# The second pass's down projection as seven half-size products, with sums of the activations formed on VectorE and GpSimd, in a replanned order

## The chip, the cores and the metric

The kernel runs on one core of a Trainium2 chip. The metric is the device time of one execution in microseconds (us). The engines are called as the profile calls them: PE (TensorE, matmuls; PEld are its weight loads), DVE (VectorE), ACT (ScalarE), POOL (GpSimd), SP (SyncE, which issues the DMAs).

## The reference, cut to what matters

```python
x = A_x                                  # (1, 1, 8192, 448)
xn = _layernorm(x, axis=-1)
s = _A_ref(xn, ...)                      # FFT along the 8192, a complex two-layer block MLP, soft threshold, inverse FFT
g = _silu((_gelu(xn @ w_gate) * (xn @ w_up)) @ w_down)   # w_gate, w_up: 448 x 1792; w_down: 1792 x 448
return x + s * g
```

All is float32 in and out. The kernel splits each float32 operand of a product into two float16 halves, hi and lo, and forms hi·hi + hi·lo + lo·hi: three matmuls for each product.

## The kernel before, in words

There are two strands of work, and both use the PE.

The feed-forward strand (`ffn`, `chunk`) takes the 8192 tokens in 16 chunks of 512 (NG = 16; a chunk is 4 tiles of 128, CH = 4), and the 1792 hidden columns as 14 blocks of 128 in **two passes**: 8 blocks in the first pass (p = 0), 6 in the second (p = 1). The weights of a pass stay in SBUF (`wt` for gate and up, `dw` for down). A chunk goes through its blocks in pairs; a pair is a **unit** (`unit`). A unit makes the gate and up products from the transposed tokens (`xta`, `xtb`, fetched by a transposing DMA) in the PSUM banks `bx` and `by`, already as seven products in place of eight (`PROD`, steps a1 to a7). ACT copies and gelu, DVE additions and `glu` give the hidden values of the unit in float32 (tiles `u` for one half of the tokens, `gl` for the other); ACT casts them to the hi part of `h`, and DVE or POOL subtracts to get the lo part. Then `down` multiplies: for each of the 4 token tiles, each block, three matmuls with 448 columns into a bank `bd`. That is 4·6·3 = 72 matmuls for a chunk of the second pass. The first pass writes its partial result to DRAM (`prt`); the second reads it back (`pt`), adds its own (DVE), takes tanh (ACT), forms the gate (DVE, tile `th`) and writes it to DRAM (`gsp`). In the last chunk the gate goes straight to the output. `ended` is this epilogue.

The spectral strand uses the banks `bf`. Phase 1 is the layer norm and the first DFT stage; phase 2 works on 64 groups (`group`: second DFT stage, the MLP, the first inverse stage; its PE groups are `bf<-sm,y`, `bf<-z,w1t`, `bf<-zs,w1t`, `bf<-w2t,wn`, `bf<-vt,sm`); phase 3 (`tiles3`, PE group `bf<-u,mt`) is the last inverse stage, multiplied with the gate read from `gsp`, added to x and written out.

The order of all instructions is made when the program is built. `Pace` runs every task as a generator, gives each instruction an estimated cost (`cost`) and lets the task go on that is due next; each engine then executes its instructions strictly in the order so found. `B` (class `Either`) gives an operation to DVE or POOL, whichever ends first by the estimates. The constants `END2` and `END3` set the even spacing at which phases 2 and 3 start their pieces. All engine calls go through one helper, so every row of the profile has the same line, L179, and groups are told apart by their tiles.

Of the kernel before, what the change touches and what calls it, by code (L numbers as in the profile page):

```python
# [21 lines left out]
NG = 16  # L22
CH = 4
# [8 lines left out]
K1, K2 = 256, 192  # L32

# [14 lines left out]
class Pace:  # L48
# [4 lines left out]
    def __init__(self):  # L53
        self.now, self.last, self.n, self.heap = 0.0, 0.0, 0, []
        self.free, self.seen, self.dma = {}, {}, 0.0

# [73 lines left out]
    def issue(self, e, op, out, ins, run):  # L130
        outs, ins, start = self.start(e, out, ins)
        if e == "SP":
            self.free[e] = start + 0.5
            size = (outs or ins)[0].nbytes()
            self.dma = max(self.dma, start) + size / 320e3
            end = max(start + 2.2 + size / (170e3 if op == "dma_start_transpose" else 240e3), self.dma + 1.5)
        else:
            end = start + self.cost(e, op, start, out, ins)
            self.free[e] = end
        for i in ins:  # L140
# [4 lines left out]
        return run()  # L145

    def cost(self, e, op, start, out, ins):

        n = max([a.free_size() for a in (out, *ins)])
        if e == "PE":  # L150
            n = out.free_size()
            return max(0.049, n * 0.00042 + 0.001) * (4 if ins[0].dtype == F32 and op == "matmul" else 1)
        if e == "ACT":
            return 0.19 + 0.00086 * n + (0.08 if op != "copy" and n > 128 else 0.0)
        if e == "POOL":
            return 1.1 if n < 8 and op == "tensor_tensor_pow" else 0.2 + 0.0023 * n
        src = [i for i in ins if i.free_size() == n]
        sb = [i for i in src if i.space != bass.MemoryType.PSUM]
        if n < 32:
# [4 lines left out]
        if op == "tensor_scalar" and sb:  # L164
            return 0.15 + 0.0008 * n + min(busy, 0.5)
        return 0.14 + 0.00107 * n
# [34 lines left out]
class Ring:  # L201
# [19 lines left out]
    def put(self, ap):  # L221
# [5 lines left out]
        else:  # L227
            self.free.append(t)

# [96 lines left out]
def afno_geglu_kernel(ctx, tc, x, gu, wd, mlp, b1, b2, c_m, c_mt, c_small, out):  # L326
# [13 lines left out]
    dsp = nc.dram_tensor("dsp", (128, 2, PF[1][1], D), F16, kind="Internal").ap()  # L340
# [87 lines left out]
    YS = ring(p1, [128, 2, 2, D], F16, "ysb", 2)  # L428
# [5 lines left out]
    XTA = ring(fp, [128, XA // 128, 256], F16, "xta", 1)  # L434
# [7 lines left out]
    PT = ring(fp, [128, D], F32, "pt", 2)  # L442
# [84 lines left out]
    def stage1(c, q, xs):  # L527
# [6 lines left out]
        for a in range(2):  # L534
# [7 lines left out]
            S.activation(ysb[:, a, 0, :], py, AF.Copy, scale=2.0 ** -16)  # L542
            yield
            V.scalar_tensor_tensor(ysb[:, a, 1, :], py, 2.0 ** -16, ysb[:, a, 0, :],
                                   op0=ALU.mult, op1=ALU.subtract)
# [3 lines left out]
        for ri in range(2):  # L549
            Q.dma_start(t1[:, ri, n2:n2 + 2, :], ysb[64 * ri:64 * ri + 64].rearrange("p a s d -> p a (s d)"))  # L550
# [57 lines left out]
    def gu_block(b, to):  # L608
# [23 lines left out]
        S.activation(fc[:, 5, b:b + 1], half[:, 1:2], AF.Copy, scale=2.0 ** -25)  # L632
# [73 lines left out]
    def down_weights(p):  # L706
# [4 lines left out]
        else:  # L711
            parts = [(fp0 + k, min(3, nf - k)) for k in range(0, nf, 3)]
# [25 lines left out]
        def split(f, n):  # L738
            t, v = yield from load(f, n)
            if p == 1:  # L740
                do = yield from WO.get()
                dv = do.rearrange("p s v c -> p (s v c)")[:, 0:2 * n * D].rearrange("p (s t c) -> p s t c", s=2, t=n)
            for i in range(n):
                d = [w[:, f + i] for w in dw] if p == 0 else [dv[:, s, i] for s in range(2)]
# [4 lines left out]
                if p == 0:  # L749
                    done("dw", f + i)  # L750
                yield
            (WS if p == 1 else rings[f]).put(t)
            if p == 1:
                Q.dma_start(dsp[:, :, f - fp0:f - fp0 + n, :], dv)
                WO.put(do)
# [18 lines left out]
        V.tensor_scalar(eguv[:, bs], eguv[:, bs], inv, 2.0 ** 14, op0=ALU.mult, op1=ALU.mult)  # L774
        V.tensor_scalar(cB[p], ED, 2.0 ** -11, None, op0=ALU.mult)
# [11 lines left out]
    def far_down():  # L787
        n = PF[1][1]
        for s in range(2):
            Q.dma_start(dw[s][:, 0:n], dsp[:, s])  # L790

    def prep_mlp():

        nonlocal f2, f20, ca, ca0, w1t, w2t, b1s, b2s
# [84 lines left out]
        rm.close()  # L879

# [40 lines left out]
    def glu(p, f0, gl, up, half, h, back):  # L921
        for cs, b in scaled(p, f0):
            V.scalar_tensor_tensor(gl[:, cs], up[:, cs], fc[:, 5, b:b + 1], gl[:, cs],
                                   op0=ALU.mult, op1=ALU.mult)
        back()
        yield
        v = gl.rearrange("p (e c) -> p e c", e=2)
# [5 lines left out]
    def unit(p, i, f0, h, xa, xb):  # L933
# [28 lines left out]
        def a2():  # L962
            m["Z"] = yield from BY.get()
            product(2, m["Z"], xb, f0, True, True)
# [10 lines left out]
        def a3():  # L975
            yield m["ep5"]
            product(3, m["Y"], xb, f0, False, True)
            pace.spawn(c12(), pace.last)

        def c12():  # L980
# [5 lines left out]
            yield m["c11"]  # L986
            yield from glu(p, f0, m["p1"], v, 0, h, lambda: V1.put(v))
# [19 lines left out]
        def a4():  # L1007
            yield m["ev2"]
            product(4, m["X"], xb, f0, False, True)
            pace.spawn(c21(), pace.last)  # L1010

        def c21():
            gl = yield from GL.get()
# [4 lines left out]
            yield from glu(p, f0, gl, m["v2"], 1, h, lambda: V2.put(m["v2"]))  # L1018
            GL.put(gl)
            done("h", p, i, f0, 1)  # L1020

        return [a1, a5, a6, a2, a3, a7], a4
# [40 lines left out]

    def pt_loads(i):
        for a in range(CH):
            t = yield from PT.get()
            Q.dma_start(t, prt[i][:, a * D:(a + 1) * D])
            yield
            EV["ptb", i, a] = t
            done("pt", i, a)  # L1070
# [21 lines left out]
    def ended(p, i, a, b, R):  # L1092
        ps = part(b, 128, D)
        if p == 0:
            th = yield from TH.get()
            S.activation(th, ps, AF.Copy, scale=cB[0])
            R.put(b)
            yield
            Q.dma_start(prt[i][:, a * D:(a + 1) * D], th)
            TH.put(th)  # L1100
            return
        yield ev("pt", i, a)
        q = EV["ptb", i, a]
        V.scalar_tensor_tensor(q, ps, cB[1], q, op0=ALU.mult, op1=ALU.add)
        R.put(b)
        yield
        th = yield from TH.get()
        S.activation(th, q, AF.Tanh)
        yield
        if i < NG - 1:  # L1110
            V.scalar_tensor_tensor(th, th, 1.0, q, op0=ALU.add, op1=ALU.mult)
            PT.put(q)
            yield
            Q.dma_start(gsp[i][:, a * D:(a + 1) * D], th)
            TH.put(th)
            if a == CH - 1:
                done("gsp", i)
            return
        yield ev("s4", a)
        s4, x4 = state["last"]  # L1120
        V.tensor_tensor(s4[:, a, :], q, s4[:, a, :], op=ALU.mult)
        V.scalar_tensor_tensor(th, th, 1.0, s4[:, a, :], op0=ALU.add, op1=ALU.mult)
        V.tensor_add(th, th, x4[:, a, :])
        PT.put(q)
        yield
        Q.dma_start(ov[:, CH * i + a, :], th)
# [50 lines left out]
    def chunk(p, i):  # L1177
        nf = PF[p][1]
        nxt = (p, i + 1) if i + 1 < NG else ((1, 0) if p == 0 else None)
        h = yield from HT.get()  # L1180
# [4 lines left out]
        yield ev("xt", "a", p, i)  # L1185
        xa = EV["xta", p, i]
        if p == 1:
            pace.spawn(pt_loads(i))
        prev = xb = None
        for u in range(nf // 2):  # L1190
            if u == 0:
                yield ev("xt", "b", p, i)
                xb = EV["xtb", p, i]
            six, last = unit(p, i, 2 * u, h, xa, xb)
            for n, s in enumerate(six):
                if n == 2 and prev:
# [8 lines left out]
        if nxt:  # L1205
# [535 lines left out]
```

## Time and profile before

| | us |
|---|---|
| median of 3 runs (1835.77 to 1837.96) | 1836.23 |
| the profiled execution's own time | 1834.92 |
| its span, first to last instruction | 1833.1 |
| PE busy | 1791.2 (98%) |
| DVE busy | 1306.3 (71%) |
| ACT busy | 1054.9 (58%) |
| POOL busy | 346.0 (19%) |

Busy times are those of the profiled execution. A matmul's end is modelled, so what one costs in a dense stretch is read from the starts of neighbours. The second pass begins at about 1005 us; phase 2 ends and phase 3 begins at about 1500 us; the last matmul starts at 1825.8 us.

### The profile page before, as it was taken

Reading aid. Unit: us, or ns where it says so; the run is one execution under the profiler, and the core shown is the slowest. Engines: PE = TensorE matmul, PEld = TensorE weight load, DVE = VectorE, ACT = ScalarE, POOL = GpSimd, SP = SyncE. Lnnn points to the kernel's source line nnn. Section 1 sums busy time; section 2 is a strip of 40 time slices with the busy share of each in tenths; the row PEclk is TensorE's granted clock in tenths of the full one; section 3 lists DMA queues with packets and bytes.
Section 4 is the critical chain, followed back from the end, with each engine's and each line's share of the span. In section 5 each row is a group of like instructions: output and inputs, shape, how many; then the busy total and the mean of one; then the engine's idle time right before and its main releaser. Section 6 shows DMA issues by size and latency. Waiting matters only on the chain. (4 is left out here: it accounts for less than half of the span.)

```text
span 1833.1 us, 36829 instructions
## 1 busy us (share of the span) xinstructions
PE 1791.2 (98%) x14785; PEld 1343.9 (73%) x14785; DVE 1306.3 (71%) x2274; ACT 1054.9 (58%) x2003; POOL 346.0 (19%) x422
## 2 busy tenths in 40 slices
PE   6999999999999999999999999999999999999998
PEld 3446667766777777887877887778877777777765
DVE  7867887777776655566766677777777766666666
ACT  4745666655655544576766766666676653333343
POOL 3434345334323123010201110101001000000000
PEclk9999999999999999999999999999999999999999
DMA  6463764866435533213236334433244349999982
GB/s 260 145 167 118 211 205 155 241 205 167 129 113 163 164 92 98 75 48 97 68 111 172 110 94 117 118 97 97 82 117 112 90 107 341 305 298 312 308 225 95
DMA packets 319196, 285.58 MB, mean 156 GB/s; under 512 B 230096, under 2 KB 286544, under 8 KB 319024
## 3 DMA queue, kind: packets, MB, share of 16 engines
q1 hardware_dynamic: 318880, 283.19, 52.5%
q8 instruction: 116, 1.90, 0.4%
q14 instruction: 56, 0.46, 0.1%
q10 hardware_dynamic: 144, 0.03, 0.0%
HBM read 128.44 MB, written 105.58 MB: 128 GB/s over the span
## 5 line engine op out<-in xcount | busy, mean ns | idle before, releaser
L179 PEld LDWEIGHTS <-wt 128*128 128x128 f16 x8582 | 834.8, 98 | 182.8 <-issue 18.1
L179 PE MATMUL bd<-dw,h 128*128 128x448 f16 x2592 | 527.9, 352 | 3.3 <-ACT th L179 2.1
L179 PE MATMUL bx<-xta,wt 128*128 128x256 f16 (+1 forms) x3843 | 474.6, 275 | 8.6 <-ACT u L179 3.9
L179 PEld LDWEIGHTS <-h 128*128 128x128 f16 x2592 | 250.1, 98 | 215.1 <-issue 4.2
L179 PE MATMUL by<-xtb,wt 128*128 128x256 f16 x2080 | 250.5, 273 | 0.9 <-ACT u L179 0.9
L179 PE MATMUL by<-xta,wt 128*128 128x256 f16 (+1 forms) x1347 | 177.7, 281 | 6.4 <-DVE wt L179 3.1
L179 ACT COPY v<-bx 128x512 f32<-128x512 f32 x208 | 121.3, 583 | 92.6 <-PE bx L179 91.7
L179 DVE TENSOR_TENSOR u<-by,u 128x512 f32<-128x512 f32 x104 | 71.5, 687 | 87.6 <-PE by L179 87.1
L179 DVE SCALAR_TENSOR_TENSOR gl<-v,fc,gl 128x512 f32<-128x512 f32 (+1 forms) x118 | 85.2, 732 | 67.7 <-ACT gl L179 67.5
L179 PE MATMUL bx<-xtb,wt 128*128 128x256 f16 x1040 | 130.6, 273 | 0.0
L179 ACT ACTIVATE u<-u,fc 128x512 f32<-128x512 f32 (+1 forms) x118 | 77.5, 669 | 67.1 <-DVE u L179 67.0
L179 POOL TENSOR_TENSOR zs<-t,zs 112x256 f16<-112x256 f32 (+2 forms) x38 | 30.9, 815 | 423.5 <-ACT zs L179 413.4
L179 ACT ACTIVATE gl<-bx,fc 128x512 f32<-128x512 f32 (+1 forms) x118 | 73.6, 637 | 64.0 <-PE bx L179 63.6
L179 ACT COPY u<-bx 128x512 f32<-128x512 f32 x104 | 60.5, 582 | 56.4 <-PE bx L179 56.3
L179 DVE SCALAR_TENSOR_TENSOR u<-v,fc,u 128x512 f32<-128x512 f32 (+1 forms) x118 | 88.4, 759 | 5.4 <-ACT u L179 1.4
L179 ACT COPY u<-by 128x512 f32<-128x512 f32 x104 | 60.8, 585 | 47.6 <-PE by L179 39.5
L179 ACT CAST h<-u 128x512 f16<-128x512 f32 x112 | 69.3, 619 | 30.0 <-DVE u L179 29.2
L179 PE MATMUL bf<-w2t,wn 112*128 112x112 f16 x1512 | 84.9, 213 | 0.0
L179 ACT ACTIVATE th<-pt 128x448 f32<-128x448 f32 x64 | 36.9, 576 | 82.9 <-DVE pt L179 82.4
L179 PEld LDWEIGHTS <-wn 112*128 112x128 f16 x1512 | 80.6, 98 | 5.2
L179 DVE SCALAR_TENSOR_TENSOR pt<-bd,fb,pt 128x448 f32<-128x448 f32 x64 | 43.6, 681 | 54.3 <-DMA pt<-prt 38.1
L179 DVE TENSOR_TENSOR v<-by,v 128x512 f32<-128x512 f32 x104 | 71.0, 683 | 11.5 <-PE by L179 10.8
(188 smaller groups left out, 2594.1 us busy)
## 6 DMA issues: line engine op xcount, KB each, us to landing
wst<-in_gu SPq DMA_DIRECT2D x22, 704.0 KB, 5.8
xts<-sx SPq DMA_DIRECT2D x32, 480.0 KB, 3.0
x<-in_x SPq DMA_DIRECT2D x17, 896.0 KB, 6.0
t<-ysb SPq DMA_DIRECT2D x64, 224.0 KB, 3.4
prt<-th SPq DMA_DIRECT2D x64, 224.0 KB, 2.3
pt<-prt SPq DMA_DIRECT2D x64, 224.0 KB, 3.7
u<-t SPq DMA_DIRECT2D x32, 448.0 KB, 5.3
y<-t SPq DMA_DIRECT2D x15, 896.0 KB, 5.0
```

The costliest lines, as they stand in the source:

```text
L179: return self.pace.issue(self.name, kind, out, ins, lambda: fn(out, *args, **kw))
```

## The change

The second pass's down projection is made as seven products in place of eight. The hidden values of a chunk are seen, for each unit, as 2 x 2 blocks (two halves of the tokens by two F blocks), `w_down` as 2 x 2 blocks (two F blocks by two halves of the 448 columns, DH = 224). Four blocks of sums of `w_down` are formed once (`factors2`), four sums of hidden values in every unit (`sums`). Each product `prod2` takes, for each of the three units, 2 token tiles and 3 hi/lo terms: 6 matmuls of 224 columns; a chunk has 7·3·6 = 126 of them. They gather in three banks; a bank's value is added to a quadrant of the result whenever it is right for one (`add2`), seven times in a chunk in place of four. The second half of a chunk's products (`tail`) is put behind the first two products of the next chunk's first unit. The sums need hidden values in float32 for longer, in slots that reuse `wt[6]` and `wt[7]`, which the second pass has free.

Around it: the second pass has two `xta` buffers and four `pt` buffers; `prt`, `gsp` and the DFT's intermediate are moved in quadrants with runs of 224 columns; phase 3 writes its output in the tile that held the gate. The planner's estimates are changed for all of the program: costs of PE, ACT, DVE and transposing DMAs, and DVE and POOL wait for each other where both would work on SBUF operands (`shares`, `port`). `END2` goes from 1440 to 1480, `END3` from 1790 to 1780. No work of the first pass and of the spectral strand is added or taken away, but their order and the choice between DVE and POOL come out differently.

```diff
+    def shares(self, e, op, out, ins):
+        n, sb, psum = self.wide(out, ins)
+        return e == "POOL" or e == "DVE" and n >= 32 and not psum and (sb >= 2 or op == "tensor_scalar" and sb > 0)
...
-        busy = max(0.0, self.free.get("POOL", 0.0) - start)
-        if len(src) >= 2 and len(sb) == len(src):
-            return 0.12 + 0.00112 * n + min(busy, 0.5 + 0.0005 * n)
...
+            t = (0.12 + 0.00112 * n if sb >= 2 else 0.15 + 0.0008 * n) + 0.06 * (extra > 0)
+        other, ahead = ("POOL", 0.15) if e == "DVE" else ("DVE", 0.0)
+        return t + max([b - start - ahead for a, b in self.port[other] if a <= start < b] + [0.0])
...
+        def sums(gl):
+            yield ev("h", p, i, f0, 0)
+            g0, x = m["g0"], gl[:, 512:768]
+            a11, a12, a21, a22 = g0[:, 0:256], g0[:, 256:], gl[:, 0:256], gl[:, 256:512]
+            B.tensor_add(x, a21, a22)
+            S.copy(h[:, f0 + 1, 0, 256:], a22)
+            yield
+            B.tensor_sub(a21, a11, a21)
+            B.tensor_sub(a11, x, a11)
+            yield
+            B.tensor_sub(a12, a12, a11)
...
+            S.copy(w[0], v)
+            yield
+            S.copy(hs[0][:, 0], g0)
+            B.tensor_sub(w[1], v, w[0])
+            B.tensor_sub(h[:, f0 + 1, 1, 256:], a22, h[:, f0 + 1, 0, 256:])
...
+            B.tensor_sub(hs[1][:, 0], g0, hs[0][:, 0])
...
+    def prod2(k, i, h, bank_, j0, j1, first=False, last=False):
...
+            for t in range(2):
+                for n, (s, v) in enumerate(((0, 0), (0, 1), (1, 0))):
+                    T.matmul(bank_[:, DH * t:DH * t + DH], w[s][:, 128 * t:128 * t + 128], right(7 * j + r, v),
...
+    def down2(i, h, last):
+        yield from last()
+        x = yield from BD.get()
+        yield from prod2(1, i, h, x, 0, 2, first=True)
+        z = yield from BY.get()
+        yield from prod2(2, i, h, z, 0, 2, first=True)
+        y = yield from BD.get()
+        yield from prod2(5, i, h, y, 0, 2, first=True)
+        yield from prod2(1, i, h, x, 2, 3)
+        e = pace.spawn(add2(i, QS[0], x), pace.last)
+        yield from prod2(2, i, h, z, 2, 3, last=True)
+        yield e
+        pace.spawn(ended2(i, QS[0], z, BY), pace.last)
+        yield from prod2(6, i, h, x, 0, 2)
...
-    END1, END2, END3 = T1 + NG * DT + 12.0, 1440.0, 1790.0
+    END1, END2, END3 = T1 + NG * DT + 12.0, 1480.0, 1780.0
```

How the order moves is shown at two places. The first is the PE where a chunk's down projection of the second pass begins (`h` are the hidden values as weights, `dw_84` and `dw_85` hi and lo of `w_down`). Before:

```order
L179 LDWEIGHTS wt_81
L179 MATMUL bx<-xta,wt_81 128x256
L179 LDWEIGHTS h
L179 MATMUL bd<-dw_84,h 128x448
L179 LDWEIGHTS h
L179 MATMUL bd<-dw_85,h 128x448
```

After:

```order
L199 LDWEIGHTS wt_81
L199 MATMUL bx<-xtb,wt_81 128x256
L199 LDWEIGHTS h
L199 MATMUL bd<-dw_84,h 128x224
L199 LDWEIGHTS h
L199 MATMUL bd<-dw_85,h 128x224
```

A matmul has half the columns and still a weight load of its own; there are 2016 of them in the program where there were 1152 of 448 columns, and the chunk's down projection now starts behind the unit's last product (`bx<-xtb`) and not before it.

The second place is the DVE in the last unit of a second-pass chunk, with phase 2's work between. Before:

```order
L179 TENSOR_TENSOR u_15138<-by,u_15138 128x512
L179 TENSOR_TENSOR h<-gl,h 128x2x256
L179 TENSOR_TENSOR v_15237<-by,v_15237 128x512
L179 TENSOR_TENSOR k_15258<-bf,k_15258 112x256
L179 TENSOR_TENSOR wn<-h_15144,wn 112x2x4x64
L179 SCALAR_TENSOR_TENSOR u_15138<-v_15237,fc,u_15138 128x512
L179 TENSOR_TENSOR v_15295<-v_15295,u_15183 128x512
L179 SCALAR_TENSOR_TENSOR u<-u,bf 128x4x112
L179 TENSOR_TENSOR wn<-h_15196,wn 112x2x4x64
L179 TENSOR_TENSOR h<-u_15138,h 128x2x256
L179 SCALAR_TENSOR_TENSOR gl<-v_15295,fc,gl 128x512
```

After (`wt_83` is the slot of the float32 hidden values and their sums, `wt_82` holds sums as weights):

```order
L199 SCALAR_TENSOR_TENSOR wt_83<-v_15398,fc,wt_83 128x512
L199 TENSOR_TENSOR wt_83<-wt_83 128x256
L199 TENSOR_TENSOR u_15423<-by,u_15423 128x512
L199 SCALAR_TENSOR_TENSOR z<-bf,z 112x512
L199 SCALAR_TENSOR_TENSOR t<-bf,t 112x256
L199 SCALAR_TENSOR_TENSOR o<-bf,ms,b2s 128x448
L199 TENSOR_TENSOR zs<-t,zs 112x256
L199 TENSOR_SCALAR c<-o,ms 128x448
L199 TENSOR_TENSOR v_15556<-v_15556,u_15444 128x512
L199 TENSOR_TENSOR v_15486<-by,v_15486 128x512
L199 TENSOR_TENSOR wt_82<-wt_83,wt_82 128x512
L199 TENSOR_TENSOR h<-wt_83,h 128x256
```

The sums (`wt_83<-wt_83`) and their lo parts (`wt_82<-wt_83,wt_82`, `h<-wt_83,h`) have come in between the unit's additions and phase 2's operations; where rows of them are missing here, POOL has them. Counted over the whole order, these operations come to: 240 new ones with 256 columns, 120 on each of DVE and POOL; of the lo parts with 512 columns 48 more than before, 15 on the DVE and 33 on POOL (shifts between the two in the first pass included); 48 more additions `pt<-bd` or `pt<-by` on the DVE; on ACT 48 more casts of 256 and 48 more of 512 columns. Between phase 3's first and last matmul stand, of all PE work, 278 us before and 260 us after, each matmul counted with the spacing of its shape in the trace.

## Rows read from the trace of the kernel before

**Rows 1.** Stages of the span: busy us (count) of each engine, clock, DMA share.

```profile
core 0: us, PE busy (x) PEld busy (x) DVE busy (x) ACT busy (x) POOL busy (x), PEclk, DMA share, GB/s
0.00:92.00 92.00, 74.60 (x378) 36.26 (x379) 76.86 (x174) 54.96 (x104) 34.78 (x46) 0.98 0.56 202
92.00:500.00 408.00, 396.87 (x2852) 278.25 (x2850) 313.79 (x551) 234.30 (x420) 162.74 (x216) 1.00 0.61 178
500.00:1005.00 505.00, 503.94 (x4389) 394.23 (x4388) 329.02 (x571) 303.66 (x590) 96.94 (x113) 1.00 0.40 110
1005.00:1500.00 495.00, 493.30 (x4781) 401.56 (x4779) 371.06 (x645) 340.48 (x686) 42.58 (x43) 1.00 0.38 100
1500.00:1800.00 300.00, 296.35 (x2210) 215.82 (x2208) 195.44 (x305) 110.64 (x188) 9.01 (x6) 1.00 0.93 291
```

**Rows 2.** PE in order of time: start, us, group and count.

```profile
1088.27 1.35 PE L179 MATMUL bf<-w2t,wn 112*128 112x112 f16 x24
1089.45 1.26 PE L179 MATMUL by<-xtb,wt 128*128 128x256 f16 x10
1090.54 1.47 PE L179 MATMUL bx<-xta,wt 128*128 128x256 f16 x12
...
1104.10 0.83 PE L179 MATMUL bf<-sm,y 128*112 128x128 f16 x12
1104.77 2.43 PE L179 MATMUL bd<-dw,h 128*128 128x448 f16 x12
1107.04 1.25 PE L179 MATMUL bx<-xtb,wt 128*128 128x256 f16 x10
```

**Rows 3.** The page's groups: weight loads of the down projection.

```profile
L179 PEld LDWEIGHTS <-h 128*128 128x128 f16 x2592 | 250.1, 98 | 215.1 <-issue 4.2
```

**Rows 4.** DVE groups by shape, 1005 to 1834 us: busy, mean ns, idle before.

```profile
L179 DVE SCALAR_TENSOR_TENSOR pt<-bd,fb,pt 128x448 f32<-128x448 f32 x64 | 43.6, 681 | 54.3 <-DMA pt<-prt 38.1 <-PE bd L179 16.0
...
L179 DVE TENSOR_TENSOR h<-gl,h 128x512 f16<-128x512 f32 x43 | 29.4, 683 | 2.7 <-ACT h L179 2.4
...
L179 DVE TENSOR_TENSOR zs<-t,zs 112x256 f16<-112x256 f32 x14 | 6.8, 488 | 2.3 <-ACT zs L179 2.3
```

**Rows 5.** POOL groups by shape, 1005 to 1834 us.

```profile
L179 POOL TENSOR_TENSOR zs<-t,zs 112x256 f16<-112x256 f32 x24 | 19.7, 823 | 230.6 <-ACT zs L179 227.3 <-issue 3.3
...
L179 POOL TENSOR_TENSOR h<-gl,h 128x512 f16<-128x512 f32 x5 | 6.3, 1261 | 103.4 <-ACT h L179 103.4
```

**Rows 6.** ACT groups by shape, 1005 to 1834 us.

```profile
L179 ACT CAST h<-gl 128x512 f16<-128x512 f32 x48 | 29.7, 619 | 9.4 <-DVE gl L179 9.2
...
L179 ACT CAST zs<-t 112x256 f16<-112x256 f32 x38 | 15.5, 407 | 8.4 <-DVE t L179 8.2
```

**Rows 7.** The window from 150 to 450 us, columns as in the first group.

```profile
150.00:450.00 300.00, 289.02 (x2165) 211.21 (x2164) 243.13 (x425) 180.78 (x326) 127.86 (x165) 1.00 0.62 185
```

**Rows 8.** POOL in order of time near 423 us.

```profile
422.85 1.78 POOL L179 TENSOR_TENSOR sx<-sf,sx 128x768 f16<-128x768 f32 x1
```

**Rows 9.** DVE in order of time there.

```profile
423.06 2.12 DVE L179 SCALAR_TENSOR_TENSOR u<-v,fc,u 128x512 f32<-128x512 f32 x1
425.11 0.34 DVE L179 TENSOR_TENSOR sf<-x,sf 128x192 f32<-128x192 f32 x1
```

**Rows 10.** DVE groups by shape, 92 to 500 us.

```profile
L179 DVE SCALAR_TENSOR_TENSOR u<-v,fc,u 128x512 f32<-128x512 f32 x18 | 17.1, 950 | 0.3
```

**Rows 11.** DVE group of the same operation, 1005 to 1834 us.

```profile
L179 DVE SCALAR_TENSOR_TENSOR u<-v,fc,u 128x512 f32<-128x512 f32 x48 | 36.6, 762 | 3.2 <-ACT u L179 1.2
```

**Rows 12.** The chain that ended last: start, us, what.

```profile
1824.35 2.59 DMA pt<-prt
1826.93 0.03 issue
...
1827.04 0.69 DVE pt L179
...
1829.13 0.62 DVE th L179
```

More of the change, by code (lines that the diff above doesn't have):

```diff
@@ L55, in __init__ @@
         self.free, self.seen, self.dma = {}, {}, 0.0
+        self.port = {"DVE": [], "POOL": []}
     def push(self, task, t):
@@ L139, in issue @@
             self.free[e] = end
+            if self.shares(e, op, out, ins):
+                self.port[e] = self.port[e][-11:] + [(start, end)]
         for i in ins:
@@ L228, in put, with __init__, get @@
             self.free.append(t)
+class Slots:
+    def __init__(self, pace, views):
+        self.pace, self.free, self.waiting = pace, [(0.0, v) for v in views], []
+    def get(self):
+        if self.free:
+            t, view = self.free.pop(0)
+        else:
+            event = Event()
+            self.waiting.append(event)
+            yield event
+            t, view = event.at
+        if t > self.pace.now:
+            yield t
+        return view
+    def put(self, view):
+        t = self.pace.ready(view, True, None)
+        if self.waiting:
+            event = self.waiting.pop(0)
+            event.at = t, view
+            self.pace.set(event)
+        else:
+            self.free.append((t, view))
 def _split(a):
@@ L711, in down_weights @@
         else:
-            parts = [(fp0 + k, min(3, nf - k)) for k in range(0, nf, 3)]
+            parts = [(f, 2) for f in range(fp0, fp0 + nf, 2)]
         def load(f, n):
@@ L986, in c12, with back @@
             yield m["c11"]
+            if p == 1:
+                g0 = m["g0"] = yield from G0.get()
+                def back():
+                    V1.put(v)
+                    U1.put(m["p1"])
+                yield from glu(p, f0, m["p1"], v, 0, h, back, g0)
+                done("h", p, i, f0, 0)
+                return
             yield from glu(p, f0, m["p1"], v, 0, h, lambda: V1.put(v))
@@ new lines, in ended2 @@
+    def ended2(i, qq, b, R):
+        yield from add2(i, qq, b)
+        if R:
+            R.put(b)
+        else:
+            done("u3", i)
+        q = EV["ptb", i, qq]
+        tf = yield from TH.get()
+        th = tf.rearrange("p (a d) -> p a d", a=2)
+        S.activation(th, q, AF.Tanh)
+        yield
+        if i < NG - 1:
+            V.scalar_tensor_tensor(th, th, 1.0, q, op0=ALU.add, op1=ALU.mult)
+            PT.put(q)
+            yield
+            Q.dma_start(blk(chunk_of(gsp, i), *qq), th)
+            TH.put(tf)
+            EV["gn", i] = EV.get(("gn", i), 0) + 1
+            if EV["gn", i] == 4:
+                done("gsp", i)
+            return
+        for a in range(qq[0], CH, 2):
+            yield ev("s4", a)
+        s4, x4 = (blk(t, *qq) for t in state["last"])
+        V.tensor_tensor(s4, q, s4, op=ALU.mult)
+        V.scalar_tensor_tensor(th, th, 1.0, s4, op0=ALU.add, op1=ALU.mult)
+        V.tensor_add(th, th, x4)
+        PT.put(q)
+        yield
+        Q.dma_start(blk(ov[:, CH * i:CH * i + CH, :], *qq), th)
+        TH.put(tf)
@@ L1093, in ended @@
         ps = part(b, 128, D)
[L1094 to L1104, printed above, removed]
+        th = yield from TH.get()
+        S.activation(th, ps, AF.Copy, scale=cB[0])
         R.put(b)
         yield
[L1107 to L1126, printed above, removed]
+        Q.dma_start(prt[i][:, a * D:(a + 1) * D], th)
         TH.put(th)
@@ L1185, in chunk @@
         yield ev("xt", "a", p, i)
+        if p == 1 and nxt:
+            pace.spawn(xt_load(nxt[1], "a", nxt[0]))
         xa = EV["xta", p, i]
@@ L1188, in chunk @@
             pace.spawn(pt_loads(i))
-        prev = xb = None
+        prev = None
         for u in range(nf // 2):
[L1191 to L1194, printed above, removed]
+            six, last = unit(p, i, 2 * u, h, xa)
             for n, s in enumerate(six):
+                if (u, n) == (0, 2) and "tail" in state:
+                    yield from state.pop("tail")()
+                if (u, n) == (0, 3):
+                    yield ev("xt", "b", p, i)
                 if n == 2 and prev:
@@ L1204, in chunk, with rest @@
         XTA.put(xa)
[L1205 removed]
+        if nxt and p == 0:
             pace.spawn(xt_load(nxt[1], "a", nxt[0]))
         cut = nf - 2
+        def rest():
+            yield from prev()
+            XTB.put(EV["xtb", p, i])
+            if (p, i) == (0, NG - 1):
+                pace.spawn(far_pair(nf // 2 - 1))
+            if nxt:
+                pace.spawn(xt_load(nxt[1], "b", nxt[0]))
+            yield pe()
+        if p == 1:
+            yield from down2(i, h, rest)
+            if not nxt:
+                yield from state.pop("tail")()
+            return
         yield from down(p, i, 0, 0, cut, hv)
         yield pe()
[L1210 to L1216 removed]
+        yield from rest()
         yield from down(p, i, 1, 0, cut, hv)
@@ L1690, in weights @@
         yield pace.spawn(down_weights(1))
-        yield pace.last + 6.0
+        yield pace.last + 5.0
+        far_rest()
+        yield pace.last + 5.0
         yield pace.spawn(prep_mlp())
```

250 lines of the change are left out of this document (173 added, 77 removed).

## The prediction

> **What bounds the kernel now.** First the stages of the span [rows 1]. The reader is to compare PE's busy time with the length of each stage: 503.9 of 505 us, 493.3 of 495, 296.4 of 300. From 500 us on the PE hardly ever waits; before that it loses 17.4 us of the first 92 and 11.1 of the next 408. Since a busy PE need not be one at its peak, the second view is the PE in order of time [rows 2], where only the starts count. In dense stretches neighbouring groups are 1.18 us apart for 24 matmuls of 112 columns (49.2 ns each), 0.67 for 12 of 128 (55.8 ns), 1.09 for 10 of 256 (109 ns), 2.27 for 12 of 448 (189.2 ns). So the spacing follows the columns, the clock is granted in full (1.00 in all these stages), and the time is the sum of the PE's columns plus 28.5 us of waits in the first 500 us and some 7 us behind the last matmul. Work taken from the PE shortens the kernel as long as the other engines keep up. The DVE is next: 371 of 495 us (75%) in the stage where phase 2 and the second pass run together, with POOL at 42.6. DMA is at 0.93 from 1500 us on, phase 3's stage.
>
> **PE, the term that carries the sum.** Removed are 16·72 = 1152 matmuls of 448 columns: 1152·0.1892 = 217.9 us. Added are 16·126 = 2016 of 224 columns. No row has 224 columns. I take the line between 128 columns (55.8 ns) and 256 (109 ns): 55.8 + 96/128·53.2 = 95.7 ns, so 192.9 us. The saving is 25.0 us, 1.56 us a chunk. Bounds: at the price per column of a 448-column matmul a matmul costs 94.6 ns, and the saving is 27.2 us. The other bound is the weight load: every matmul still has its own, 98 ns in the page [rows 3], and if it were not hidden, 2016·0.098 = 197.6 us leave a saving of 20.3 us. I take 25.0, as 24 matmuls with as many loads in 1.18 us show that a load isn't waited for.
>
> [...]
>
> **DVE, POOL and ACT, the cost.** In the order 240 operations of 256 columns are new, 120 on each of DVE and POOL; nearest rows are `zs<-t,zs`, 488 ns on the DVE [rows 4] and 823 ns on POOL [rows 5]. Of the lo parts with 512 columns the DVE gets 15 more (683 ns [rows 4]), POOL 33 (1261 ns [rows 5]). The additions into `pt` grow by 48 (681 ns [rows 4]). DVE: 58.6 + 10.2 + 32.7 = 101.5 us, 6.3 a chunk. POOL: 98.8 + 41.6 = 140.4 us, 8.8 a chunk. ACT: 48·0.407 + 48·0.619 = 49.2 us [rows 6], 3.1 a chunk, on an engine at 69% in the fullest of these stages [rows 1]; it is hidden there. Had the vector work no cover, 101.5 us would show four times over what the PE saves; the cover is the DVE's idle quarter. In the 1005 to 1500 us stage nine chunks lie: DVE 371 + 57 = 428 us, POOL 42.6 + 79 = 122 us, and the stage shrinks to 495 - 14 = 481 us. The DVE is then at 89%, POOL at 25%.
>
> What the DVE's queue delays reaches the PE: behind a late sum stand, in order, the next unit's `u<-by`, which frees a bank for the PE, and phase 2's `z<-bf`, which frees a `bf` bank. The rows give both ends of the price. In this stage now, at 75%, the PE loses 1.7 of 495 us. From 150 to 450 us, with the DVE at 81% and POOL at 43%, it loses 11.0 of 300 us, 3.7% [rows 7]. For 481 us that is 0 or 16 us more than now. I take 7: the DVE is fuller than in either, POOL far less busy than in the second, and the products that need the sums are put behind 60 matmuls (5.7 us) and two products of the next chunk (24 matmuls of 109 ns, 2.6 us), where a chain of sums takes two casts and five subtractions, about 5 us by the rows above.
>
> **The estimates.** They move no work between PE and the rest, but change the order in the first pass too. Their point shows at 423 us: POOL works from 422.85 for 1.78 us [rows 8], and a DVE operation on SBUF operands that starts at 423.06 takes 2.12 us [rows 9] where its mean is 0.76 in the later stages [rows 11] and 0.95 in the POOL-heavy one [rows 10]. The old estimate caps this wait. What can come back is at most the 11.1 us lost between 92 and 500 us [rows 1], and at worst a new order loses a few more; I take -4, between nothing and all, nearer nothing because several of these waits have to do with PSUM and casts. [...]
>
> **Ends.** The last addition waited for its `pt`, fetched at 1824.35 and landed at 1826.93 [rows 12], 1.1 us after the last matmul began. Four `pt` buffers are filled when the chunk begins; I take -1 (0 to -2). The new sums of `w_down` are made once, in the first pass: for each of three units 7 subtractions and 4 ACT operations, where 12 operations in all are dropped. Nothing waits for them before the second pass, so other work hides them; uncovered, at the rows' prices, they are 10 to 15 us.
>
> **Sum.** 1834.9 (the profiled execution, span 1833.1 and 1.8 around it) - 25.0 - 1 + 7 - 4 = 1811.9; this execution was 1.3 us under the median of the runs, so 1813 us.
>
> **Rivals.**
>
> A, the forecast: the PE's columns go, the other engines keep up nearly. 1804 to 1820. Chance 0.50.
>
> B, the estimates do more: the PE's waits of the first pass go, and the second pass gets none. 1836.2 - 26 - 11 = 1799. For it speaks that the PE's later stages show waits can be planned away; against it the DVE at 89%. Chance 0.14.
>
> C, the second pass waits as the window from 150 to 450 us does: +16 in place of +7, and nothing saved in the first pass: 1813 + 9 + 4 = 1826. Chance 0.17.
>
> D, phase 3 runs into the DMA. Its stage holds 0.93·300 = 279 us of DMA; phase 3's matmuls stand within 260 us of PE work where they had 278, so about 282 us remain, 99%. Runs of 224 columns are half as long as before; what that costs no row here prices. If everything took 5% more, 293 us would want to go into 282: +11, 1824. Against it: loads are asked for two pieces ahead. Chance 0.06.
>
> E, weight loads set the pace at 98 ns: a saving of 20.3 in place of 25, 1818; by the bare row of loads [rows 3], against which the 49.2 ns speak. Chance 0.03. [...]
>
> F, the other side: DVE and POOL shut each other out so much that they set the pace from 1005 to 1500 us. The DVE's 428 us plus what it stands still for POOL must pass 481 for that: 53 us, 43% of POOL's 122. The gain of 26 is gone when it stands still for 79 us, 65%; were every microsecond of POOL one of the DVE's, the stage would be 550 us and the kernel 1836 - 26 + 69 = 1879. For it: `u<-v,fc,u` takes 25% longer at POOL's 40% share [rows 10, 11]; scaled to POOL's 25% and to that part of the DVE's work that has only SBUF operands, which I put at half, that is 16% of 214, 34 us, short of 53 but near. Against it: operations that read PSUM don't wait, and the order now foresees such waits. Chance 0.09, with 1840 to 1860 as its middle.
>
> **How the numbers follow.** The likeliest case gives 1813. From 1797 to 1832 the range holds A, B, C, D and E but for their far ends, 0.84 or so; outside are F and what goes wrong together in C. A measurement of this kernel tells about 0.2% (3.7 us) from no change: faster means under 1832.5, slower over 1839.9. A, B, D, E and most of C are faster: 0.88; the 0.01 just named, the upper end of C and the mild end of F are the same: 0.04; the rest of F is slower: 0.08.
>
> **What would show it.** Right: a dense run of 12 `bd` matmuls of 224 columns 1.15 us from start to start of the next group; PE idle in the second pass below 10 us in all; the last `pt` addition not waiting for a DMA; DVE near 89 to 93% in phase 2's part of the second pass. Wrong: 224-column matmuls at 98 ns or more; DVE at 97% or more there with PE gaps that end on DVE or POOL sums (`wt`, `h`); PE waits for `u` or `mt` DMAs after 1480 us; a first pass that loses more than 11 us after the first 92.

## The result, and the profile after

The changed kernel takes 1840.15 us (median of 20 runs, 1836.73 to 1845.24), the kernel before 1837.99 beside it (20 runs): ratio 1.0016, 95% interval [1.0009, 1.0023]. That is 2 to 3 us slower, inside the 0.2% that counts as no change, and 27 us over the forecast. The profiled execution of the changed kernel has a span of 1838.16 us, 5.0 more than before (1833.14).

The stages of the span after, columns as in [rows 1]:

```profile
0.00:92.00 92.00, 72.34 (x351) 34.34 (x352) 70.42 (x164) 50.81 (x97) 25.50 (x34) 0.94 0.55 194
92.00:500.00 408.00, 398.24 (x2856) 279.80 (x2855) 324.41 (x602) 240.21 (x426) 143.18 (x188) 1.00 0.63 183
500.00:1005.00 505.00, 504.09 (x4385) 394.38 (x4383) 336.81 (x608) 307.80 (x595) 69.01 (x89) 1.00 0.40 108
1005.00:1500.00 495.00, 491.71 (x5308) 449.29 (x5306) 419.72 (x726) 362.74 (x743) 155.62 (x152) 1.00 0.45 109
1500.00:1800.00 300.00, 285.72 (x2521) 245.94 (x2519) 236.06 (x360) 126.86 (x224) 74.34 (x74) 0.99 0.91 283
```

The PE still fills phase 2's stage (491.7 of 495 us), but in the last one it is busy for 285.7 of 300 us where it was for 296.4 [rows 1]. The matmuls themselves cost what was forecast. The PE in order of time, in phase 2's stage:

```profile
1107.48 0.73 PE L199 MATMUL bf<-vt,sm 128*128 128x448 f16 x3
1108.05 1.31 PE L199 MATMUL bd<-dw,h 128*128 128x224 f16 x12
1109.20 1.02 PE L199 MATMUL by<-dw,h 128*128 128x224 f16 x9
```

Twelve matmuls of 224 columns take 1.15 us from start to start, 96 ns each. So the gain on the PE is there, and something gives it back. To find where, I took the time from each matmul's start to the next one's. Where it is more than 80 ns over the median of its shape, I added up all that lies over the median, and call this the PE's **gaps**; the medians themselves add up to 1773.4 us before and 1749.2 after.

| us | gaps to 100 | 100 to 1000 | 1000 to 1500 | from 1500 | last start to end of span |
|---|---|---|---|---|---|
| before | 18.0 | 16.1 | 2.0 | 4.7 | 7.3 |
| after | 23.2 | 14.3 | 5.3 | 25.9 | 8.4 |

The differences (-24.2 of medians, +5.2, -1.8, +3.3, +21.2, +1.1, and 0.5 in gaps under 80 ns) make up the 5.0 us of the span to within 0.3 us. The gaps of a kernel are those of one execution. Seven of the runs below (e3, e4, e5, e6, e9, e10, e13) issue their matmuls in the changed kernel's order up to about 1040 us, and their gaps from 100 to 1000 us are 16.4 to 18.5 us where the changed kernel's are 14.3; so 4 us in one band can be chance. The loss is in phase 3's stage, where 4.7 us became 25.9. What the PE waited for from 1500 us, by releaser (us in total, times, longest), after:

```profile
PE bd L199 <- DVE pt L199: 6.1, 15, 1.4
PE bd L199 <- DVE h L199: 4.2, 5, 1.4
PE bx L199 <- ACT v L199: 3.4, 1, 3.4
PE bd L199 <- ACT h L199: 1.2, 1, 1.2
PE bd L199 <- POOL h L199: 1.1, 1, 1.1
PE bf L199 <- DMA mt<-c_mt: 0.7, 1, 0.7
PE bx L199 <- ACT u L199: 0.4, 1, 0.4
```

and before:

```profile
PE bx L179 <- ACT u L179: 2.3, 2, 1.8
PE by L179 <- ACT u L179: 0.9, 1, 0.9
PE bf L179 <- DMA mt<-c_mt: 0.3, 1, 0.3
```

The down projection (`bd`) now waits for hidden values (`h`), and for an addition (`pt`) that reads a bank before the next product may accumulate into it. The longest single wait is of another kind. `bx` waits 3.4 us for ACT's copy `v`, and ACT has itself stood still before that copy (start, us, engine, group, and in brackets the idle time before it and its releaser):

```profile
1558.25 1.47 PE L199 MATMUL by<-xta,wt 128*128 128x256 f16 x12
1562.04 0.58 ACT L199 ACTIVATE th<-pt 128x448 f32<-128x448 f32 x1 [6.01 <-DMA gsp<-th]
1562.53 0.57 ACT L199 COPY v<-bx 128x512 f32<-128x512 f32 x1
1563.14 2.29 PE L199 MATMUL bx<-xtb,wt 128*128 128x256 f16 x10 [3.42 <-ACT v L199]
```

ACT's tanh (`th<-pt`) needs one of the two `th` buffers, and the write of the gate from it (`gsp<-th`), issued at 1552.7 us, landed after 9.3 us, where the median of these writes is 3.3. In ACT's order the copy stands behind the tanh. So this wait goes back to a DMA, and no sum is in its chain.

Now a place where the PE waits for `h`, the rows that matter of all engines:

```profile
1674.40 1.25 PE L199 MATMUL bx<-xtb,wt 128*128 128x256 f16 x10
1674.87 0.68 DVE L199 SCALAR_TENSOR_TENSOR g<-bf,ms,g 128x448 f32<-128x448 f32 x1
1675.46 0.68 DVE L199 TENSOR_TENSOR v<-v,u 128x512 f32<-128x512 f32 x1
1675.49 1.31 PE L199 MATMUL bd<-dw,h 128*128 128x224 f16 x12
1675.68 1.48 POOL L199 TENSOR_TENSOR wt<-wt,wt 128x512 f16<-128x512 f32 x1 [1.47 <-ACT wt L199]
1676.06 1.65 DVE L199 TENSOR_TENSOR wt<-wt,wt 128x512 f16<-128x512 f32 x1
1677.63 0.61 DVE L199 TENSOR_TENSOR g<-g,x 128x448 f32<-128x448 f32 x1
1678.17 0.68 DVE L199 TENSOR_TENSOR v<-by,v 128x512 f32<-128x512 f32 x1
1678.36 1.31 PE L199 MATMUL bd<-dw,wt 128*128 128x224 f16 x12
1679.43 0.74 DVE L199 SCALAR_TENSOR_TENSOR wt<-v,fc,u 128x512 f32<-128x512 f32 x1
1680.20 0.93 ACT L199 CAST h<-wt 128x512 f16<-128x512 f32 x2 [1.69 <-DVE wt L199]
1680.87 0.37 PE L199 MATMUL bd<-dw,h 128*128 128x224 f16 x2 [1.20 <-ACT h L199]
1681.34 1.21 DVE L199 TENSOR_TENSOR h<-wt,h 128x512 f16<-128x512 f32 x1
1682.61 0.93 PE L199 MATMUL bd<-dw,h 128*128 128x224 f16 x4 [1.37 <-DVE h L199]
1683.33 1.33 PE L199 MATMUL by<-dw,h 128*128 128x224 f16 x6
```

The chunk's last unit ends on the PE at about 1675.5. Its addition `v<-by,v` starts on the DVE only at 1678.17: ahead of it stand the lo part of a sum (`wt<-wt,wt`, 1.65 us, while POOL works on SBUF operands too) and phase 3's work. The multiplication, the cast and the lo part follow, and `h` is there at 1682.6. The PE has 36 matmuls to do meanwhile and then stands still twice. The last row shows a second price: six matmuls of 224 columns in 1.33 us. The clock of the stretch (windows, columns as in [rows 1]):

```profile
1560.00:1566.50 6.50, 3.36 (x17) 2.34 (x17) 2.08 (x4) 3.23 (x6) 0.00 (x0) 0.74 1.05 400
1682.50:1686.00 3.50, 3.40 (x19) 2.78 (x20) 2.37 (x6) 0.74 (x3) 0.73 (x1) 0.52 0.98 156
1820.00:1826.00 6.00, 3.69 (x24) 2.83 (x23) 3.38 (x5) 0.00 (x0) 1.19 (x1) 0.72 0.12 38
```

Granted is 0.52 of the full clock right after the two waits. The first window is that of the 3.4 us wait, the third follows waits of 1.13 and 1.17 us. By their starts, the matmuls of the three slow stretches took 1.6, 1.6 and 1.4 us more than at the medians of their shapes, some 4.5 of the 21 us. Before the change the clock is 1.00 in these three windows.

### The profile page after: what moved, and what is told of

Its sections match the earlier page's. It is cut to its first block, busy times and chain, and to the rows that moved or that the text cites. A ratio compares the mean times of both kernels' runs of the same rounds, so it can differ in the third digit from the quotient of the medians.

```text
span 1838.2 us, 39083 instructions
## 1 busy us (share of the span) xinstructions
PE 1779.2 (97%) x15649; PEld 1427.1 (78%) x15649; DVE 1417.2 (77%) x2503; ACT 1100.8 (60%) x2105; POOL 477.4 (26%) x544
## 5 line engine op out<-in xcount | busy, mean ns | idle before, releaser
L199 PEld LDWEIGHTS <-wt 128*128 128x128 f16 x9350 | 911.3, 98 | 188.0 <-issue 23.3
L199 PEld LDWEIGHTS <-h 128*128 128x128 f16 x2688 | 257.8, 98 | 139.4 <-DVE h L199 8.5
L199 PE MATMUL bd<-dw,h 128*128 128x448 f16 (+1 forms) x1920 | 346.6, 329 | 8.3 <-DVE h L199 5.7
L199 POOL TENSOR_TENSOR wt<-wt 128x256 f32<-128x256 f32 x94 | 77.3, 823 | 285.0 <-DVE wt L199 263.4
L199 PE MATMUL bd<-dw,wt 128*128 128x224 f16 (+1 forms) x816 | 97.1, 268 | 6.0 <-DVE pt L199 6.0
L199 POOL TENSOR_TENSOR zs<-t,zs 112x256 f16<-112x256 f32 (+1 forms) x36 | 30.7, 852 | 267.9 <-ACT zs L199 254.4
L199 ACT CAST h<-wt 128x512 f16<-128x512 f32 (+1 forms) x128 | 68.5, 537 | 37.6 <-DVE wt L199 25.1
L199 DVE SCALAR_TENSOR_TENSOR pt<-bd,fb,pt 128x448 f32<-128x448 f32 x96 | 64.0, 678 | 27.3 <-PE bd L199 26.8
L199 ACT ACTIVATE th<-bd,fb 128x448 f32<-128x448 f32 x62 | 39.2, 632 | 71.9 <-PE bd L199 50.1
```

The source lines that it names most:

```text
L199: return self.pace.issue(self.name, kind, out, ins, lambda: fn(out, *args, **kw))
```

## The experiments

Three theories to begin with. **S**: the vector work for the sums makes the DVE late where a unit ends. **R**: the new estimates give a worse order. **M**: phase 3, packed more tightly by `END2` and `END3`, runs into the DMA or itself. All ratios are to the kernel before, run beside it on the same chip. Every edit is planned anew, so behind the place that it names the rest of the order can shift too.

### One part alone

**e1_estimates_only**: the kernel before with only the class `Pace` of the change.

```diff
+    def shares(self, e, op, out, ins):
...
+        other, ahead = ("POOL", 0.15) if e == "DVE" else ("DVE", 0.0)
+        return t + max([b - start - ahead for a, b in self.port[other] if a <= start < b] + [0.0])
```

> The kernel before with the changed kernel's cost estimates and nothing else (eight products, old END2 and END3). Theory S (the vector work for the sums makes the DVE late at the ends of units, and the PE waits for it after 1500 us): the estimates alone are worth little, 1833 to 1843 us. Rival R (the replanned order costs it: later start, worse places in the first pass): the 25 us that were lost show here too, 1850 us or more. Rival M (phase 3 packed more tightly runs into the DMA): no change, 1836 to 1840, as phase 3 keeps its spacing.

1839.64 us, 1.0011 [1.0002, 1.0019]. Gaps to 100 us 22.1 in place of 18.0. The estimates alone lose 2 us, at the start.

**e2_old_estimates**: the changed kernel with the old `Pace`.

> The changed kernel planned with the old cost estimates. S: the sums remain and are planned worse, 1838 to 1860 us, with PE waits on DVE after 1500 us as large as with the new estimates or larger. R: the saving of the matmuls shows, 1810 to 1820 us. M: 1835 to 1842 us.

1846.19 us, 1.0044 [1.0029, 1.0058]. The gaps to 100 us are back at 17.8, but they are 22.6 from there to 1000 us (14.3 in the changed kernel, up to 18.5 in other runs with its order) and 36.4 from 1000 us on (31.2). So the new estimates cost at the start and help by more behind it; R holds for the first 100 us only.

**e3_no_sums**: no sums from the second chunk on; products 3 to 7 read other numbers there.

```diff
         def sums(gl):
...
+            if i > 0:
...
+                S.copy(w[0], v)
+                yield
+                B.tensor_sub(w[1], v, w[0])
...
+                return
```

> The changed kernel with the sums of hidden values left out in all chunks of the second pass but the first: a unit makes one cast and one subtraction of 512 columns there, as many as the kernel before, and the PE multiplies what stands in the slots. S: the PE's waits after 1500 us fall from some 26 us with their clock drops to under 8, and the time is 1812 to 1822 us. R and M: the waits stay, 1833 to 1842 us.

1822.11 us, 0.9915 [0.9902, 0.9927]; gaps from 1500 us 7.1. Planned without the sums, the kernel is 18 us faster: S. The long wait behind `gsp<-th` goes with them: ACT still waits for these writes, up to 4.2 us, but from 1500 us on the PE waits for `pt` alone.

**e7_old_ends**: `END2`, `END3` back at 1440 and 1790 in the changed kernel.

> The changed kernel with the planned ends of the second and third phase as before (1440 and 1790 in place of 1480 and 1780). Theory M (the third phase's work, packed into 295 us, fills DVE and the queues beside the second pass): less DVE work a microsecond after 1500 us, PE gaps there from 26 to under 15 us, 1828 to 1834 us, with some more gaps between 1005 and 1440. Theory S (the sums alone): the loss only moves to earlier chunks, 1836 to 1846 us.

1845.85 us, 1.0046 [1.0029, 1.0062]; gaps 12.5 between 1000 and 1500 us, 23.6 from there. The gaps from 1500 us hardly fall and the earlier ones grow: M falls as the main cause. Nearest to it is the wait behind `gsp<-th`, 3.4 us and the slow stretch after it; in e7 `bx` waits only 0.7 us for `v`, and the kernel is slower still.

### What of the sums costs: waiting for them, or making them

**e9_sums_unread**, **e10_unread_pool** and **e13_unread_dve** make all sums, but products 3 to 7 read the plain halves of products 1 and 2 (so the second pass's values differ); **e5_sums_dve** and **e6_sums_pool** read them as the change does. The edits, and the names after them for the engine that has the sums:

```diff
-                yield ev("hs", i, 2 * j, e)
-                w = [left2(h, j, s)[:, e, c:c + 256] for s in range(2)]
+                yield ev("h", 1, i, 2 * j, 0)
+                w = [h[:, 2 * j + e, s, 0:256] for s in range(2)]
...
-            B.tensor_add(x, a21, a22)
+            V.tensor_add(x, a21, a22)
```

> The changed kernel with every sum and cast still made by the same engines, but the five products that read sums (3 to 7) read the plain halves that products 1 and 2 read, so TensorE waits for no sum; the second pass's products are then not the reference's from the first chunk on. It splits theory S in two. S-load (the sums fill DVE and Pool, so that the last unit's own multiplication and subtraction, and the additions to the partial sums, come late): the waits on h and pt stay, 1834 to 1842 us. S-latency (products stand still for the sums themselves): the loss goes as it did without the sums, 1820 to 1826 us, with DVE and Pool as busy after 1500 us as in the changed kernel.

> The changed kernel with all sums on DVE, none on Pool. If it is the mutual waiting of DVE and Pool that makes the units' ends late, Pool's share falls to that of the kernel without sums (11 us between 1500 and 1800) and the time falls to 1825 to 1834 us. If it is the sheer amount of DVE work, DVE goes from 79 to about 90% or more between 1500 and 1800 us, and the time rises to 1845 to 1875 us.

> The changed kernel with all sums on Pool, none on DVE. If DVE's amount of work is the cause, DVE falls by the sums that it holds now and the time falls to 1825 to 1836 us. If it is the length of the chain of sums (Pool takes 0.8 us for 256 and 1.4 us for 512 elements against 0.53 and 1.06 on DVE) or the mutual waiting, the time rises to 1845 to 1880 us, the PE waiting on POOL's writes of h.

> As the run whose products 3 to 7 read plain halves and wait for no sum (1832.3 us; its sums and casts are all made, on DVE and Pool; the second pass's products are not the reference's), but with all sums on Pool. It takes the sums' load from DVE and leaves the mutual waiting of the two engines. If DVE's amount of work makes what is left of the loss, the time falls to 1820 to 1827 us; if the mutual waiting makes it, it stays at 1830 us or goes above.

> As the run whose products 3 to 7 read plain halves and wait for no sum (1832.3 us, sums on DVE and Pool) and the one with the sums on Pool (1834.1), now with all sums on DVE. If DVE's amount of work makes the part of the loss that is not waiting for sums, the time rises to 1842 us or more, with DVE above 82% between 1500 and 1800. If it is the two engines' waiting for each other, it falls to 1822 to 1828 us.

| sums on | read: us, ratio | made, not read: us, ratio |
|---|---|---|
| DVE and POOL, as planned | 1840.15, 1.0016 [1.0009, 1.0023] | 1832.31, 0.9974 [0.9962, 0.9986] |
| DVE | 1859.96, 1.0117 [1.0100, 1.0134] | 1846.45, 1.0050 [1.0035, 1.0066] |
| POOL | 1845.90, 1.0044 [1.0029, 1.0059] | 1834.07, 0.9985 [0.9976, 0.9994] |
| nowhere (e3) | | 1822.11, 0.9915 [0.9902, 0.9927] |

Reading the sums takes some 8 of the 18 us (first row), making them some 10; e9's time lies between the ranges of its two theories. The 8 are not simply products that stand still for sums. In the changed kernel's trace only `bd<-wt,h`, in the last chunk, waits for sums, 1.4 us in all from 1500 us on; the other waits for `h`, 5.1 us, are `bd<-dw,h`, which needs plain hidden values. The wait behind `gsp<-th` and the three slow stretches are absent from e9's trace; what else the 8 hold isn't shown. Of the 10 neither theory gets all. All sums on the DVE cost 24 us unread, so its amount of work counts (254.7 of 300 us busy in the last stage). But with the DVE free of them the time isn't better than with the planner's choice. What stands against a gain is seen in DVE groups by shape, 1500 to 1800 us (busy, mean ns). Without sums:

```profile
L199 DVE TENSOR_TENSOR g<-g,x 128x448 f32<-128x448 f32 x53 | 32.9, 620 | 0.7
L199 DVE TENSOR_TENSOR h<-wt,h 128x512 f16<-128x512 f32 x28 | 21.9, 786 | 0.3
L199 DVE TENSOR_TENSOR u<-by,u 128x512 f32<-128x512 f32 x21 | 14.5, 689 | 12.4 <-PE by L199 12.4
L199 DVE TENSOR_TENSOR v<-v,u 128x512 f32<-128x512 f32 x20 | 13.8, 688 | 3.9 <-ACT v L199 3.9
```

With all sums on POOL, unread:

```profile
L199 DVE TENSOR_TENSOR g<-g,x 128x448 f32<-128x448 f32 x54 | 46.3, 862 | 0.7
L199 DVE TENSOR_TENSOR v<-v,u 128x512 f32<-128x512 f32 x19 | 17.6, 927 | 2.2 <-ACT v L199 2.1
L199 DVE TENSOR_TENSOR h<-wt,h 128x512 f16<-128x512 f32 x18 | 16.8, 932 | 1.5 <-ACT h L199 1.4
L199 DVE TENSOR_TENSOR u<-by,u 128x512 f32<-128x512 f32 x20 | 13.7, 686 | 11.9 <-PE by L199 11.9
```

The DVE does none of the sums, POOL is busy for 145.2 of the 300 us where it was for 11.0 without sums, and the three operations shown that have two SBUF operands take 19 to 39% longer; the one that reads PSUM (`u<-by,u`) takes 686 ns where it took 689. So part of POOL's work is paid for on the DVE. How the 10 us divide between the DVE's own work and this isn't settled.

### The order of the products

**e4_late_last_unit**: the parts of products 1 and 2 that need the chunk's last unit, and with them the first part of product 6 (which accumulates onto product 1's bank), go behind the next chunk's first two products, to the start of `tail`.

```diff
-        yield from prod2(1, i, h, x, 2, 3)
-        e = pace.spawn(add2(i, QS[0], x), pace.last)
-        yield from prod2(2, i, h, z, 2, 3, last=True)
...
         def tail():
+            yield from prod2(1, i, h, x, 2, 3)
+            e = pace.spawn(add2(i, QS[0], x), pace.last)
+            yield from prod2(2, i, h, z, 2, 3, last=True)
...
```

> The changed kernel with the parts of products 1, 2 and 6 that need a chunk's last unit moved behind the first two products of the next chunk (2.6 us of matmuls more as cover for the last unit's hidden values; 36 matmuls stay ahead). S: the waits for h at a chunk's end get shorter, 1828 to 1836 us. R and M: no change, 1838 to 1842 us.

1833.48 us, 0.9982 [0.9972, 0.9991]; gaps from 1500 us 9.0, between 1000 and 1500 us 12.2. The same work, some 6 us less. From 1500 us on `bd` waits for DVE's `h` for 1.4 us where it was 4.2, and for `pt` for 3.0 where it was 6.1. The wait behind `gsp<-th` and the slow stretches are gone as well, so the later products are not all of these 17 us. Some comes back earlier: between 1000 and 1500 us `bf` waits 4.9 us for phase 2's `k`, where it was 2.1.

**e8_late_unit_early_old**: the same, planned with the old estimates up to 100 us.

```diff
...
+        if start < 100.0:
+            return self.early(e, op, start, out, ins)
```

> The kernel whose products of the last unit come after the next chunk's first two (e4_late_last_unit), planned with the estimates of the kernel before until 100 us of planned time and with the new ones from there. If the new estimates cost some 4 us in the first pass's start alone (as the run with the estimates alone and this kernel's sibling say: PE gaps of 22 us before 100 us against 18), it gives 1827 to 1831 us; if the order of the start has nothing to do with it, 1832 to 1836 us.

1827.18 us, 0.9942 [0.9924, 0.9960]; gaps to 100 us 18.3. Windows of the start, the changed kernel and then this one:

```profile
50.00:65.00 15.00, 11.54 (x45) 4.65 (x44) 11.87 (x29) 10.57 (x24) 5.08 (x4) 0.66 0.44 128
```

```profile
50.00:65.00 15.00, 13.36 (x64) 5.96 (x63) 12.49 (x41) 14.36 (x31) 4.60 (x4) 0.89 0.29 83
```

In the changed kernel the PE is busy for 11.5 us in place of 13.4, at a clock of 0.66 in place of 0.89 (the kernel before has 13.4 and 0.89 too, e4 has 11.2 and 0.77). This is R's part.

**e11_late_old_ends**: e8 with the old ends.

> e8_late_unit_early_old (1827.2 us) with the planned ends of the second and third phase as before the change (1440 and 1790). Its PE gaps are now 12 us between 1100 and 1500 and 12 us after 1500 us, so by theory S this trades one for the other: 1825 to 1832 us. By theory M it is faster, 1818 to 1824 us.

1829.47 us, 0.9958 [0.9941, 0.9975]: no gain, as for e7.

**e12_split_tail**: e8, with products 6, 3, 7 and 4 one product further back.

```diff
-            yield e
             pace.spawn(ended2(i, QS[0], z, BY), pace.last)
+            state["tail2"] = lambda: tail2(e)
+
+        def tail2(e):
+            yield e
             yield from prod2(6, i, h, x, 0, 2)
...
```

> The fastest kernel so far (e8_late_unit_early_old, 1827.2 us) with the rest of the down projection cut in two: products 6, 3, 7 and 4, which accumulate into a bank that DVE is still adding to a partial sum, come after the third product of the next chunk's first unit. If the waits for these additions (4.9 us after 1000 us) cost TensorE their own length, they go and the time falls to 1821 to 1825 us; if another wait takes their place, it stays at 1826 to 1830 us.

1816.50 us, 0.9889 [0.9875, 0.9904], **1.1% faster than the kernel before**. Its waits of the PE from 1000 us on:

```profile
PE bd L225 <- DVE pt L225: 2.9, 8, 0.8
PE bx L225 <- ACT v L225: 1.7, 2, 1.1
PE bd L225 <- DVE h L225: 1.4, 2, 1.0
PE bf L225 <- DMA mt<-c_mt: 1.1, 2, 1.0
```

The stage from 1500 us, as in [rows 1]:

```profile
1500.00:1800.00 300.00, 293.87 (x2631) 254.16 (x2629) 246.91 (x396) 132.75 (x240) 79.42 (x75) 1.00 0.90 285
```

The DVE is busier than in the changed kernel (246.9 against 236.1 us) and the PE too. Gaps: 3.1 between 1000 and 1500 us (12.1 in e8) and 10.4 from 1500 us. The time fell by some 10 us, more than the 4.9 us of waits that the move was to take. The waits for `k`, 4.8 us in e8, are gone too, though the edit does not name them; how much of the 10 us is the move itself and how much the new order around it isn't shown.

**e15_split_later**: both parts one product later still.

> e12_split_tail with both parts of the rest of the down projection one product later (before the fourth and the fifth of the next chunk's first unit). If sums and multiplication still come late there (h 2.3 us and pt 2.9 us of TensorE's waits after 1000 us), it gives 1812 to 1816 us; if what is left are waits of other kinds, or the next unit's sums are pushed back by it, 1816 to 1822 us.

1829.64 us, 0.9964 [0.9953, 0.9974]. A new wait:

```profile
PE by L225 <- DVE pt L225: 9.4, 11, 2.2
```

Product 2 gathers in a `by` bank, which the next unit's own product now wants before the addition has read it.

**e14_split_no_sums**: e12 without the sums, as e3.

> The fastest kernel (e12_split_tail, 1816.5 us) without the sums from the second chunk on, one cast and one subtraction of 512 columns in their place (products 3 to 7 then read other numbers). In the changed kernel leaving them out gave 18 us. If the late order hides them, it gives 1812 to 1816 us; if most of their cost is DVE's and Pool's load, which the order does not take away, 1798 to 1808 us.

1809.15 us, 0.9852 [0.9836, 0.9867]. That is between the two ranges. In this order the sums cost 7 us, in the changed kernel's 18: the order hides more than half.

## Why the prediction was wrong, by its steps

**PE, 25.0 us.** Right: 96 ns for 224 columns against 95.7, 24.2 us in the medians. Every matmul has a load of its own (15649 of each on the page after), and it isn't waited for: 24 matmuls of 112 columns (`bf<-w2t,wn`), whose loads the page gives at 98 ns each, take 1.18 us from start to start (1086.06 to 1087.24), 49 ns each. So rival E is out. A slip without consequence: the prediction reads a clock of 1.00 in all stages, and the first has 0.98 [rows 1].

**The vector work's amount.** In the stage from 1005 to 1500 us the DVE has 419.7 us (85%) where 428 and 89% were forecast, POOL 155.6 (31%) where it was 122 and 25%. The DVE was right, POOL's forecast was a fifth too low. The DVE's sum was right with luck: a lo part `wt<-wt,wt` of 512 columns takes 924 ns on it from 1000 us on, not the 683 of the price, and POOL has taken over other work (`g<-g,x`, 12 of 60 from 1500 us on, where it had 2).

**+7 for the PE's waits.** This is the step that failed: +24.5 came. It was priced for 1005 to 1500 us alone, where it was +3.3. For phase 3's stage, which had 7 more chunks with the same sums, the sum had no term, and no reason was given (the DVE was at 65% there [rows 1]). There +21.2 came, with the DVE at 79%. Three things were wrong in it. A stage's share says little about a chain that must end on time: the DVE was idle for a fifth of this stage, and the unit's `v<-by,v` still queued for 2.7 us behind other work. And the cover was counted for the wrong chain. The 60 matmuls and the next chunk's products lie ahead of products that need *sums*; products 1 and 2 need the last unit's plain `h`, and have 36 matmuls ahead, 3.5 us. Its chain (addition, multiplication, cast, lo part) is lengthened by lo parts of sums that stand before it on the DVE. And the additions `pt`, seven a chunk, were priced as work of the DVE but not as waits: the PE stood 15 times, 6.1 us in all, until one had read its bank. By the trace from 1500 us on, the waits for plain `h` are 5.1 us, for `pt` 6.1, for sums 1.4, the one behind `gsp<-th` 3.4, and the slow stretches some 4.5; none of these had a term for this stage. e4 and e12 show from the other side that the order decides: some 6 us and then, from e8, some 10 come back with the same work, by moving products and replanning around them.

**-4 for the estimates.** Wrong in sign for the first pass: +5.2 to 100 us (e1, e8), and the -1.8 between 100 and 1000 us is less than executions of one order differ by. What they are worth behind that shows only beside the new sums (e2: 4 to 8 us from 100 to 1000 us and 5 from there).

**Ends, -1.** The last addition no longer waits for a DMA, but from the last matmul's start to the end of the span it is 8.4 us, not 7.3. In the trace the last addition starts at 1832.45 us, 2.7 us after the last matmul began, behind other quadrants' work on the DVE.

**Rivals.** The time fell at the lower edge of F. Its mechanism shows on the DVE's side: the 19 to 39% above, e10 beside e3. That operations which read PSUM don't wait shows for one of them: in the kernel before `u<-by,u` takes 684 ns from 92 to 500 us, with POOL at 40%, and 688 from 1005 us on, with POOL at 6%. But it was put in the wrong place, and its condition, a DVE that sets the pace at 97%, was not needed. C had the nearest size (+16 where +24.5 came), at the wrong stage. B's second pass without waits is what e14 comes near to. The chance of 0.01 counted under "the same" was the author's estimate for weight loads that take the gain away; no run shows such loads, and the runs show 96 ns for 224 columns and 24.2 us of gain in the medians. D's sign, the PE waiting for `mt`, is 0.7 us, but a DMA, the late write of the gate, reached the PE by another way, through ACT: 3.4 us and 1.6 of slow clock. No run takes that wait out alone; e7, without it, is no faster.

**Signs.** The 1.15 us for twelve matmuls came true. The PE's gaps in the second pass are 31.2 us, not below 10. Of the signs for "wrong", gaps that end on `h` came, but with the DVE at 85% and not at 97%, and `mt` was waited for by 0.7 us. Dear matmuls and a worse first pass behind its start did not come.

## What to carry to other kernels

Work moved from the PE to a vector engine must be costed along the chain that the PE waits for next, with what stands ahead of it in that engine's queue, not by the engine's share of a stage. When such a change gives nothing, leave its extra work out once: if the gain appears, look for another order before giving the change up; here the order of the same work decided some 16 us (e4 and e12), more than half of what the product saves. Follow a wait back more than one step: the longest one here named ACT, and ACT was waiting for a DMA. And a product may be put back only until the bank that it holds is wanted by someone else.

## What was not expected of the hardware

After a wait of 3.4 us that ended at 1563.1 us the granted clock was 0.50 from 1563 to 1566 us; after waits of 1.20 and 1.37 us within 3 us at 1681 it was 0.50 from 1683 to 1685; the matmuls behind took 1.6 us more each time. A third stretch at 0.50, from 1823 to 1825 us, followed waits of 1.13 and 1.17 us. From 1500 to 1800 us the changed kernel has a mean granted clock of 0.99, e12 one of 1.00.
